# Attention rows of five batches turned into columns through DRAM and DMA transposes in a fused attention and MLP kernel

## The chip, the cores and the metric

The kernel runs on one core of one Trainium2 chip. The metric is the device time of one execution in microseconds (us), as the median of several runs. The core has five engines that run side by side and meet only at semaphores: PE (TensorE, matrix products into eight PSUM banks), ACT (ScalarE), DVE (VectorE), POOL (GpSimd) and SP (SyncE). SP computes nothing here. It issues DMAs, one after the other, and an instruction of SP that waits for a semaphore holds back every DMA behind it. POOL issues DMAs too, on a queue of its own. All DMAs share the core's 16 DMA engines.

## What is computed

Causal attention over 8 batches of 8 heads (576 rows, 64 columns each): the first four heads see the last 32 rows, the other four see every fourth row of the last 128. Its output, 4608 tokens of 512 features, goes through an MLP with 2048 hidden features and a gated activation.

```python
# _attn_ref
scores = scale * np.matmul(q, k.transpose(0, 1, 3, 2))
mask_plain = (rel >= 0) & (rel < window)
mask_dil = (rel >= 0) & (rel < window * dilation) & (rel % dilation == 0)
...
scores = np.where(masks[None, :, :, :], scores, -1000000000.0)
...
attn = attn / (np.sum(attn, axis=-1, keepdims=True) + 1e-09)
return np.matmul(attn, v).astype(np.float32)

# _moe_ref
h = x @ w_in
g = h * (1.0 / (1.0 + np.exp(-beta * h)))
return (g @ w_out).astype(np.float32)
```

## The kernel before

The products run in bf16. The MLP needs the attention output as columns: features on the partitions, tokens along the free axis. That tile is `xT`, 128 partitions by 4 feature blocks `x` (two heads each) by 4608 tokens. Blocks 0 and 1 hold the plain heads, blocks 2 and 3 the dilated ones.

**The MLP** goes over nine token tiles `t` of 512 tokens. For each of 16 blocks of hidden features, `slot_h` makes a slot of four matmuls (L683) from `xT` into a bank, ACT takes its tanh (L690) and DVE multiplies the gate into `g` (L695). `block` then makes the output for 128 tokens in four parts of four matmuls each (L710), ACT or DVE evacuates it to `osb` (L728, L730), and SP stores it (L735). I call a group of four matmuls h*t.n* or o*t.n*: h3.0 is the first slot of tile 3, o2.7 the eighth group of tile 2's output. At most three banks are held by h groups and two by o groups.

**The attention** of a batch makes 14 score groups S (L554, L559, L565), each followed by an exponential on ACT (L592) and, from batch 3 on, by a mask product on POOL or DVE (L604). Then come 12 value groups V (L624), whose rows DVE normalises into a tile `xs` (reciprocal L636, product L637). There are eight `xs` tiles per batch, one for each block `x` and half `j` of the 576 tokens. The function `back` transposes an `xs` tile on PE against the identity (L651, three transposes of 96 rows or four of 72), and `put` copies the bank into `xT` (L205, a helper that serves all copies), on ACT or DVE. The transposes of a batch are named X.

**Loads.** Batches 0 to 2 load q, k and v directly. For batch b from `DIRECT = 3` on, POOL issues two casting DMAs (q and k from float32 to a bf16 DRAM scratch `s`), and SP issues three loads of v (tile `st`, L335) and four DMA transposes from the scratch into `dk`, `dq` and twice `raw` (`crossbar`, L386). POOL and DVE spread these into `qzd`, `kz`, `qd`, `vd` and `vp`. The casts wait for a gate of tile b-2 and for the transposes of batch b-1.

**The order of the work** on every engine is written out in advance by `Plan.run`. Each step has dependencies, estimated costs on the engines that could run it, and a due time `vt` in units of token tiles. The planner keeps a clock for each engine, one for the DMA system and one for each bank, and of the steps that can start within some tens of nanoseconds of the first it takes the one with the earliest due time. A DMA step is counted as landed 1100 ns after its turn in the DMA system. On the chip the planner's times play no part, only the order it chose: every engine runs its list strictly in sequence. Batch b's attention is due during tile b-1, and tile b's h groups need columns of batch b and some of batch b-1. A tile 3 group reads all of batch 3's columns; from tile 4 on, tile t needs only the first half (j = 0) of batch t, beside columns of batch t-1.

Of the kernel before, what the change touches and what calls it, by code (L numbers as in the profile page):

```python
# [9 lines left out]
BF16 = mybir.dt.bfloat16  # L10
# [144 lines left out]
def kernel(  # L155
# [10 lines left out]
    nc = tc.nc  # L166
    P = 128
    B, H, S, D = q.shape
# [6 lines left out]
    C = 4  # L175
# [4 lines left out]
    QT = 96  # L180
# [6 lines left out]
    DIRECT = 3  # L187
# [4 lines left out]
    dram_pool = ctx.enter_context(tc.tile_pool(name="dram", bufs=1, space=bass.MemoryType.DRAM))  # L192
# [4 lines left out]
    plan = Plan(range(8))  # L197
# [6 lines left out]
    def copy(e, out, in_):  # L204
# [15 lines left out]
    xT = const([P, NKT, B * S], BF16, "xT")  # L220
# [6 lines left out]
    xs = {(x, j): const([QT if x < 2 else HT, 3 if x < 2 else C, 2, D], BF16, f"xs{x}{j}")  # L227
          for x in range(4) for j in range(2)}
# [172 lines left out]
    def used(key, o):  # L401
        last.setdefault(key, []).append(o)

    def wrote(*keys):
        for key in keys:
            last[key] = []

    xcopy = {}

    def attention(b, ld, names, vts):  # L410

        steps = {}
# [2 lines left out]
        if b < DIRECT:  # L415
            for n in [x for x in names if x[0] in "KQ"]:
                z, kind, i = "KQ".index(n[0]), n[1], int(n[2])
                vt = vt_of[n]
                g = Group("a")
                if kind == "P":  # L420
# [4 lines left out]
                    r = plan.op([("DVE", 480), ("POOL", 1000), act(1024)], relay, deps, vt)  # L425
                    wrote(("rl", z, i))
                    used(("st", z), r)
                    pieces = [rl[:, z, i, T].rearrange("p h d -> p (h d)") for T in range(R)]
                    tdep = [r]
                else:  # L430
                    src = (ks, qs)[z]
                    pieces = [src[:, 4 + h, (4 * c + 2 * i) * D:(4 * c + 2 * i + 2) * D]
                              for h in range(4) for c in range(2)]
# [32 lines left out]
        else:  # L466
            vt = vt_of["zPRE"]
            ready = {"D": [ld["x", 0, 4]]}
            ops = []
            for hf in range(2):  # L470
                def spread(e, hf=hf):
                    rows = slice(64 * hf, 64 * hf + 64)
                    copy(e, qzd[kv][rows, hf], dq[rows])
                o = plan.op([("DVE", 900), ("POOL", 1150)], spread,
                            [ld["x", 1, 4], late_fill, fill4] + war(("qzd", kv, 0), ("qzd", kv, 1)), vt)
# [5 lines left out]
            for e_ in range(2):  # L481
# [4 lines left out]
                o = plan.op([("POOL", 1200), ("DVE", 1400)], spread, [ld["x", 0, 0], late_fill] + war("kz"), vt)  # L486
# [17 lines left out]
        vt = vt_of["zVAL"]  # L504
# [137 lines left out]
        for name in [n for n in names if n[0] == "X"]:  # L642
            x, j = int(name[1]), int(name[2])
            vt = vt_of[name]
            n, m = (QT, 3) if x < 2 else (HT, 4)
            g = Group("a")

            def back(e, x=x, j=j, g=g, n=n, m=m):
                xp = bank(g, BF16)
                for a in range(m):  # L650
                    nc.tensor.transpose(  # L651
                        xp[:, a * n:(a + 1) * n], xs[x, j][:, a].rearrange("p h d -> p (h d)"),
                        ident_b[0:n, 0:n])
            need = [vdone[x, j]] if x < 2 else [vdone[x, 2 * j], vdone[x, 2 * j + 1]]
            xop = plan.op([("PE", m * mm(n))], back, need, vt, acquire=g)
            wrote(("xs", x, j))
            used(("xs", x, j), xop)

            def put(e, x=x, j=j, g=g):
                xp = bank(g, BF16)[:, 0:S // 2]  # L660
                o = xT[:, x, b * S + j * S // 2:b * S + (j + 1) * S // 2]
                if x >= 2:
                    copy(e, o.rearrange("p (t r) -> p t r", r=C), xp.rearrange("p (r t) -> p t r", r=C))
                elif b < DIRECT:
                    copy(e, o, xp)
                else:
                    copy(e, o.rearrange("p (i m e) -> p i m e", i=3, e=2),
                         xp.rearrange("p (i e m) -> p i m e", i=3, e=2))
            xcopy[b, x, j] = plan.op([act(S // 2), dve(S // 2)], put, [xop], vt - .002, group=g)
# [181 lines left out]
```

## Time and profile before

| | |
|---|---|
| runs | 328.39, 328.99, 329.13 us; median 328.99 us |
| profiled execution | 328.01 us, of which the span of recorded instructions is 326.3 us |
| granted TensorE clock | 1.0 |
| PE | 311.8 us busy, 96% of the span |
| DVE, ACT, POOL | 218.4, 190.2, 107.0 us busy |
| DMA moved | 40.03 MB |

The profile comes from one execution. A page gives busy times by engine, the chain of work that ended last (followed back from the last instruction to whatever released each step), the costliest groups of instructions, and the DMA issues with their time to landing. PE's busy time counts pipelined matmuls, so the chain is the safer reading of what PE takes. "SPq" rows are DMA instructions on SP's queue: their duration is how long SP was held by the instruction, not how long the data took.

### The profile page before, as it was taken

The page shows a single profiled execution, that of the slowest core. Times are in us where ns is not written, and L with a number is a line of the kernel's source. Part 1 is how long each engine was busy: PE and PEld are TensorE (multiplying, and loading weights), DVE is VectorE, ACT ScalarE, POOL GpSimd, SP SyncE. Part 2 cuts the span into 40 slices and gives each one's busy share as a digit, 9 for nine tenths or more (in the row PEclk, how much of TensorE's full clock was granted, in tenths as well). Part 3 has the DMA queues.
Part 4 walks back from the last instruction along what each step waited for, and adds up shares of the span by engine and source line. Part 5 has one row for each costly group of instructions (what it writes and reads, how often), then busy time and mean ns, then how long its engine had stood idle before and what let it go on. Part 6 is the DMA issues. An engine that isn't in the chain of part 4 may idle for free.

```text
span 326.3 us, 6475 instructions
## 1 busy us (share of the span) xinstructions
PE 311.8 (96%) x2445; PEld 176.7 (54%) x2485; DVE 218.4 (67%) x500; ACT 190.2 (58%) x365; POOL 107.0 (33%) x135
## 2 busy tenths in 40 slices
PE   6888999999999998999999999999999999999994
PEld 4766777566555544555555455545554444444441
DVE  5577678778787868887789768876885344344300
ACT  3677778587666656464746574657464544445411
POOL 7999352603542539045405520551000000000000
PEclk9999999999999999999999999999999999999999
DMA  6999999979606892899489457950000010000111
GB/s 85 180 208 208 203 156 176 148 164 228 99 33 140 213 182 87 183 242 167 104 210 188 121 104 176 220 125 32 34 32 34 32 64 35 32 32 34 57 72 64
DMA packets 69614, 40.03 MB, mean 123 GB/s; under 512 B 50816, under 2 KB 64272, under 8 KB 69264
## 3 DMA queue, kind: packets, MB, share of 16 engines
q0 software_dynamic: 20784, 16.09, 35.0%
q1 hardware_dynamic: 48800, 23.54, 32.2%
q8 instruction: 19, 0.31, 0.4%
q14 instruction: 11, 0.09, 0.1%
HBM read 40.37 MB, written 15.34 MB: 171 GB/s over the span
## 4 chain that ended last, share of the span: by engine, by line
PE 85%; DVE 4%; ACT 3%; DMA 3%; issue 2%; POOL 1%; SPq 1%; POOLq 0%; ACTq 0%; DVEq 0%
PE bank L710 36%; PE bank L683 34%; PE bank L624 4%; PE bank L651 3%; PE bank L554 2%; PE bank L394 2%; PE bank L548 2%; PE bank L565 2%; DMA st<-in_k_dram 2%; DMA raw<-s 1%; ACT tnh L690 1%; DVE xs L637 1%; DVE g L695 1%; SPq L386 1%; POOL qd L205 1%
## 5 line engine op out<-in xcount | busy, mean ns | idle before, releaser
L690 ACT ACTIVATE tnh<-bank,beta_half 128x512 bf16<-128x512 f32 (+2 forms) x160 | 102.6, 644 | 90.2 <-PE bank L683 81.8
L683 PE MATMUL bank<-xT,w_in_bf 128*128 128x512 bf16 (+2 forms) x621 | 144.2, 357 | 1.9 <-ACT xT L205 0.3
L710 PE MATMUL bank<-w_out_bf,g 128*128 128x512 bf16 x555 | 141.6, 379 | 1.1
L695 DVE SCALAR_TENSOR_TENSOR g<-tnh,bank 128x512 bf16<-128x512 bf16 (+2 forms) x160 | 100.6, 632 | 60.9 <-ACT tnh L690 59.0
L683 PEld LDWEIGHTS <-w_in_bf 128*128 128x128 bf16 x640 | 58.3, 97 | 49.3 <-issue 2.5
L710 PEld LDWEIGHTS <-g 128*128 128x128 bf16 x576 | 52.2, 98 | 50.3
L592 ACT ACTIVATE pt<-bank 128x288 bf16<-128x288 f32 (+1 forms) x112 | 44.9, 446 | 5.4 <-PE bank L554 2.1
L637 DVE TENSOR_TENSOR xs<-bank,rcp 72x256 bf16<-72x256 f32 (+1 forms) x96 | 44.6, 465 | 3.3
L604 POOL TENSOR_TENSOR pt<-pt,mask_d 128x288 bf16<-128x288 bf16 x15 | 12.0, 808 | 66.9 <-ACT pt L592 66.8
L728 ACT ACTIVATE osb<-bank 128x512 f32<-128x512 f32 (+1 forms) x35 | 20.7, 591 | 17.5 <-PE bank L710 16.6
L624 PEld LDWEIGHTS <-pt 128*128 128x128 bf16 x448 | 22.6, 97 | 12.1 <-issue 0.7
L651 PEld LDWEIGHTS <-xs 72*128 72x128 bf16 (+1 forms) x224 | 15.3, 97 | 13.0 <-DVE xs L637 1.4
L651 PE MATMUL bank<-ident_b,xs 72*128 72x72 bf16 (+1 forms) x224 | 18.8, 200 | 1.2 <-DVE xs L637 0.8
L636 DVE RECIPROCAL rcp<-bank 72x4 f32<-72x4 f32 (+1 forms) x96 | 16.8, 175 | 4.0 <-PE bank L624 2.6
L205 DVE COPY xT<-bank 128x288 bf16<-128x288 bf16 x31 | 13.5, 437 | 7.4 <-PE bank L651 7.3
L205 ACT COPY xT<-bank 128x288 bf16<-128x288 bf16 x33 | 13.1, 397 | 8.4 <-PE bank L651 8.3
L554 PE MATMUL bank<-qzd,dk 128*128 128x144 bf16 x128 | 17.7, 232 | 0.0
L624 PE MATMUL bank<-vd,pt 128*128 128x65 bf16 x256 | 16.2, 193 | 0.3
L205 POOL CAST vd<-st 80x1024 bf16<-80x1024 f32 (+1 forms) x10 | 10.5, 1052 | 15.6 <-DMA st<-in_v_dram 15.2
L554 PEld LDWEIGHTS <-dk 128*128 128x128 bf16 x128 | 11.6, 101 | 5.3 <-issue 0.6
L205 POOL COPY qd<-raw 64x1152 bf16<-64x1152 bf16 x10 | 12.3, 1231 | 1.8 <-PE bank L651 1.6
L604 DVE TENSOR_TENSOR pt<-pt,mask_d 128x288 bf16<-128x288 bf16 x25 | 10.7, 450 | 1.1 <-ACT pt L592 1.1
(96 smaller groups left out, 227.0 us busy)
## 6 DMA issues: line engine op xcount, KB each, us to landing
out_dram<-osb SPq DMA_DIRECT2D x35, 256.0 KB, 2.2
st<-in_v_dram SPq DMA_DIRECT2D x5, 768.0 KB, 8.5
s<-in_k_dram POOLq DMA_DIRECT2D x5, 576.0 KB, 5.6
s<-in_q_dram POOLq DMA_DIRECT2D x5, 576.0 KB, 8.3
st<-in_v_dram SPq DMA_DIRECT2D x5, 512.0 KB, 6.0
w_out_bf<-in_moe_w_out_dram POOLq DMA_DIRECT2D x2, 1024.0 KB, 21.7
st<-in_k_dram POOLq DMA_DIRECT2D x6, 288.0 KB, 9.1
st<-in_q_dram POOLq DMA_DIRECT2D x6, 288.0 KB, 10.6
```

The lines of the kernel that those rows point to most:

```text
L205: (nc.scalar.copy if e == "ACT" else E[e].tensor_copy)(out=out, in_=in_)
L554: nc.tensor.matmul(sc[:, a, 0:2 * n], lhsT=dk[kv][:, rp, h4, hf * (CT - P):hf * (CT - P) + P], rhs=qzd[kv][:, :, rp, h4, hf * HT:(hf + 1) ...
L592: nc.scalar.activation(out=pt_of(x, j, n).rearrange("p (a b) n -> p a b n", a=2), in_=sc[:, :, 0:2 * n].rearrange("p a (b n) -> p a b n", ...
L604: E[e].tensor_tensor(out=w, in0=w, in1=m, op=ALU.mult)
L624: nc.tensor.matmul(pv[:, a, h2, :], lhsT=pt[x][:, c], rhs=rhs, start=True, stop=True)
L637: nc.vector.tensor_tensor(out=xs[x, jx][:, a0:a0 + m], in0=pv[0:n, :, :, 0:D], in1=rc[0:n, 0:m].unsqueeze(3).to_broadcast([n, m, 2, D]), o ...
L651: nc.tensor.transpose(xp[:, a * n:(a + 1) * n], xs[x, j][:, a].rearrange("p h d -> p (h d)"), ident_b[0:n, 0:n])
L683: nc.tensor.matmul(bank(g)[:, 0:n], lhsT=w_in_bf[:, kt, fb * P:(fb + 1) * P], rhs=xT[:, kt, xo:xo + n], start=(kt == 0), stop=(kt == NKT - 1))
L690: nc.scalar.activation(out=th[:, 0:n], in_=bank(g)[:, 0:n], func=ACT.Tanh, scale=beta_half[:, fb:fb + 1])
L695: nc.vector.scalar_tensor_tensor(out=g_t[t % 2][:, fb, c0:c0 + n], in0=th[:, 0:n], scalar=1.0, in1=bank(g)[:, 0:n], op0=ALU.add, op1=ALU.mult)
L710: nc.tensor.matmul(bank(g), lhsT=g_t[t % 2][:, fb, tb * P:(tb + 1) * P], rhs=w_out_bf[:, fb, :], start=(fb == 0), stop=(fb == NFB - 1))
L728: nc.scalar.mul(out=ob[:, cols], in_=bank(g)[:, cols], mul=0.5)
```

## The change

For batches 3 to 7, `back_dma` takes the place of `back` and `put`. An `xs` tile is stored to a DRAM scratch of 288 rows of 128 bf16 (73.7 KB): one store for blocks 2 and 3, two stores for blocks 0 and 1, where even and odd rows lie in different halves of the partitions. Then a DMA transpose brings the scratch into `xT`, after both stores have landed. Both kinds are issued by SP. Batches 0 to 2 keep PE's way. Per batch that is 12 stores and 8 DMA transposes more on SP, 28 PE transposes (8 X groups) and 8 copies fewer; over five batches 60 stores, 40 DMA transposes, 140 PE transposes and 40 copies.

```diff
+    def back_dma(b, x, j, vt, vdone):
+
+        rows = dram_pool.tile([S // 2, P], BF16, name=f"x{b}_{x}{j}")
+        if x < 2:
+            to = rows[:].rearrange("(i m e) c -> e m i c", e=2, m=QT // 2)
+            pieces = [(xs[x, j][e * QT // 2:(e + 1) * QT // 2].rearrange("p a h d -> p a (h d)"), to[e])
+                      for e in range(2)]
+            need = [vdone[x, j]]
+        else:
+            pieces = [(xs[x, j][:].rearrange("p r h d -> p (r h d)"),
+                       rows[:].rearrange("(t r) c -> t (r c)", r=C))]
+            need = [vdone[x, 2 * j], vdone[x, 2 * j + 1]]
+        wrote(("xs", x, j))
+        out = []
+        for src, dst in pieces:
+            o = plan.op([("SP", 450)], lambda e, s=src, d=dst: nc.sync.dma_start(out=d, in_=s), need, vt,
+                        dma=74 * 1000 / len(pieces) / 200)
+            used(("xs", x, j), o)
+            out.append(o)
+        cols = xT[:, x, b * S + j * S // 2:b * S + (j + 1) * S // 2]
+        xcopy[b, x, j] = plan.op(
+            [("SP", 600)], lambda e: nc.sync.dma_start_transpose(out=cols.unsqueeze(1), in_=rows[:]), out,
+            vt, dma=74 * 1000 / 200)
 
     def attention(b, ld, names, vts):
...
         for name in [n for n in names if n[0] == "X"]:
             x, j = int(name[1]), int(name[2])
             vt = vt_of[name]
+            if b >= DIRECT:
+                back_dma(b, x, j, vt, vdone)
+                continue
             n, m = (QT, 3) if x < 2 else (HT, 4)
```

Since the planner runs again, the order moves too, from batch 3 on. In the changed kernel the lines after L409 lie further down: tanh is L717, the evacuation L755, the exponential L616, the store of the output L762, the new store L425 and the new DMA transpose L431.

ACT's list shows where tile 3 begins. Each tanh row is one h group, each `pt` row one S group, each `osb` row four o groups. Before, from the evacuation of o1.11 on (the ninth row is the tanh of h3.0):

```order
L728 ACTIVATE osb_98<-bank_66 128x512
L690 ACTIVATE tnh_92<-bank_70,beta_half 128x512
L205 COPY xT<-bank_67 128x288
L690 ACTIVATE tnh_93<-bank_66,beta_half 128x512
L205 COPY xT<-bank_69 128x288
L690 ACTIVATE tnh_94<-bank_67,beta_half 128x512
L690 ACTIVATE tnh_95<-bank_66,beta_half 128x512
L728 ACTIVATE osb_99<-bank_68 128x512
L690 ACTIVATE tnh_92<-bank_67,beta_half 128x512
L592 ACTIVATE pt_110<-bank_66 128x4x72
L690 ACTIVATE tnh_93<-bank_69,beta_half 128x512
L592 ACTIVATE pt_111<-bank_66 128x4x72
```

The same place now:

```order
L755 ACTIVATE osb_98<-bank_65 128x512
L717 ACTIVATE tnh_92<-bank_68,beta_half 128x512
L717 ACTIVATE tnh_93<-bank_70,beta_half 128x512
L717 ACTIVATE tnh_94<-bank_68,beta_half 128x512
L717 ACTIVATE tnh_95<-bank_70,beta_half 128x512
L755 ACTIVATE osb_99<-bank_71 128x512
L616 ACTIVATE pt_110<-bank_70 128x4x72
L616 ACTIVATE pt_111<-bank_65 128x4x72
L616 ACTIVATE pt_110<-bank_66 128x4x72
L616 ACTIVATE pt_111<-bank_67 128x4x72
L755 ACTIVATE osb_96<-bank_68 128x512
L616 ACTIVATE pt_110<-bank_65 128x4x72
```

The copies into `xT` are gone, and the tanh of h3.0 has moved behind 17 further rows: batch 4's 14 exponentials and three evacuations (o2.3, o2.7, o2.11). After it 13 tanh rows of tile 3 follow one another. The beginnings of tiles 5 and 6 have moved back in the same way, by a few groups of the tile before and some of the next batch's scores. Tiles 7 and 8 alternate h and o as before.

SP's list at the loads of batch 4, before:

```order
L735 DMA out_dram<-osb_96 128x512
L735 DMA out_dram<-osb_97 128x512
L335 DMA st_120<-in_v_dram 80x4x256
L335 DMA st_120<-in_v_dram 128x4x256
L335 DMA st_121<-in_v_dram 128x24x64
L386 DMA_TRANSPOSE dk_129<-s_0_138 128x2x576
L386 DMA_TRANSPOSE dq<-s_1_139 128x2x576
L386 DMA_TRANSPOSE raw<-s_0_138 128x1x1152
L386 DMA_TRANSPOSE raw<-s_1_139 128x1x1152
```

And now (x_20 is the scratch of block 2, half 0):

```order
L762 DMA out_dram<-osb_96 128x512
L425 DMA x_20_138<-xs_116 72x512
L425 DMA x_30_139<-xs_118 72x512
L335 DMA st_120<-in_v_dram 80x4x256
L335 DMA st_120<-in_v_dram 128x4x256
L335 DMA st_121<-in_v_dram 128x24x64
L431 DMA_TRANSPOSE xT<-x_20_138 128x1x288
L386 DMA_TRANSPOSE dk_129<-s_0_146 128x2x576
L386 DMA_TRANSPOSE dq<-s_1_147 128x2x576
L386 DMA_TRANSPOSE raw<-s_0_146 128x1x1152
L386 DMA_TRANSPOSE raw<-s_1_147 128x1x1152
L431 DMA_TRANSPOSE xT<-x_30_139 128x1x288
```

Two new stores stand ahead of batch 4's loads and one new DMA transpose ahead of its crossbar transposes; the store of `osb_97` has moved behind them. The other columns of batch 3 follow after that: 14 more of the new DMAs and three stores of the output, and then, last:

```order
L762 DMA out_dram<-osb_96 128x512
L425 DMA x_20_148<-xs_116 72x512
L762 DMA out_dram<-osb_97 128x512
L431 DMA_TRANSPOSE xT<-x_01_144 128x1x288
L431 DMA_TRANSPOSE xT<-x_11_145 128x1x288
```

Here batch 3's last two DMA transposes, which h3.0 waits for, stand behind a store of batch 4's rows (x_20_148) and behind the store of the output groups o2.4 to o2.7 (`osb_97`). Before, nothing of the kind stood on SP there: from `raw` to batch 5's loads its list had three stores of the output.

## The prediction

> **What bounds the kernel now.** I read the page's busy times first, then its chain that ended last.
>
> ```profile
> PE 311.8 (96%) x2445; PEld 176.7 (54%) x2485; DVE 218.4 (67%) x500; ACT 190.2 (58%) x365; POOL 107.0 (33%) x135
> PE 85%; DVE 4%; ACT 3%; DMA 3%; issue 2%; POOL 1%; SPq 1%; POOLq 0%; ACTq 0%; DVEq 0%
> ```
>
> PE holds 85% of the chain, so a group of matmuls taken off PE is worth its full time unless something else is late. Whether something is late differs by stage, so next I asked for busy times in stretches of 15 us (columns: PE, PEld, DVE, ACT, POOL, clock, DMA share, GB/s).
>
> ```profile
> 120.00:135.00 15.00, 13.99 (x100) 7.28 (x100) 12.51 (x24) 9.27 (x18) 9.53 (x10) 1.00 0.65 132
> 165.00:180.00 15.00, 14.84 (x131) 8.29 (x133) 13.73 (x34) 8.60 (x17) 4.60 (x5) 1.00 1.03 203
> 180.00:195.00 15.00, 14.89 (x101) 7.76 (x102) 10.85 (x23) 9.12 (x18) 6.48 (x7) 1.00 0.45 109
> 255.00:270.00 15.00, 14.89 (x69) 6.80 (x70) 5.71 (x10) 7.38 (x11) 0.00 (x0) 1.00 0.09 35
> ```
>
> In the stages that the change touches PE is busy 14.84 to 14.89 us of 15, as it is in the stage without attention (255 to 270), with one exception: about 0.9 us are lost between 120 and 135. DVE and ACT are never full. So PE binds, and every reduction of its work counts.
>
> **What the change takes off PE.** The chain in order of time has the X groups one by one (start, us, what).
>
> ```profile
> 160.30 0.17 PE bank L565 x4
> ...
> 173.10 0.12 PE bank L554 x2
> ...
> 175.29 0.12 PE bank L624 x4
> ...
> 180.41 0.13 PE bank L651 x4
> 180.55 0.86 PE bank L683 x4
> 181.41 0.13 PE bank L651 x3
> 181.54 0.19 PE bank L624 x6
> ```
>
> An X group takes 0.13 us between its neighbours, whether of four 72-row or three 96-row transposes, and an h group 0.86 (S groups take 0.12 or 0.17, V groups 0.12 or 0.19; I use these below). Eight X groups in each of five batches are 40 x 0.13 = 5.2 us. All lie on the bounding engine: I take -5.2.
>
> **The copies.** The 40 copies into `xT` cost some 0.4 us each, 17 us in all:
>
> ```profile
> L205 DVE COPY xT<-bank 128x288 bf16<-128x288 bf16 x31 | 13.5, 437 | 7.4 <-PE bank L651 7.3
> L205 ACT COPY xT<-bank 128x288 bf16<-128x288 bf16 x33 | 13.1, 397 | 8.4 <-PE bank L651 8.3
> ```
>
> ACT and DVE have that time free beside PE, so I count 0. What hides it is PE's work; should another engine set the pace, the copies' absence helps by at most that one's share.
>
> **What it adds: SP.** SP gets 60 stores and 40 DMA transposes. The stores' nearest row is the store of the output, which holds SP 332 ns and lands in 2.0 us; for the new DMA transposes it is `raw`, four times their size.
>
> ```profile
> L735 SPq DMA_DIRECT2D out_dram<-osb x37: 332/332/537, 58.4 to 322.7; - x37
> L386 SPq DMA_TRANSPOSE raw<-s x10: 1194/1530/3010, 81.0 to 211.4; - x10
> L386 SPq DMA_TRANSPOSE dk<-s x5: 5582/5694/9456, 73.8 to 201.9; - x5
> L386 SPq DMA_TRANSPOSE dq<-s x5: 1247/1304/2507, 79.5 to 208.4; - x5
> DMA to landing us min/median/max: 1.7/2.0/8.1
> raw<-s SPq DMA_TRANSPOSE x10, 4.1
> ```
>
> (The three figures are minimum, median and maximum in ns; the last two rows give us to landing, of the output's stores and of `raw`.) A store I take at 0.35 us of SP and 2 us to landing. A DMA transpose of 74 KB lies between a quarter of `raw` (0.3 to 0.4 us) and all of it (1.5 us). I take 0.4, because SP's time on `raw` goes with the data: 295 KB in 1.3 us is 227 GB/s, about the rate at which the DMA engines run at that time. Landing I take at 2.5 us, between the quickest store, 1.7, and `raw`, 4.1, which are the ends, and nearer the former by its size.
>
> The row that worries me is `dk`: the same size as `dq`, yet SP is held 5.7 us instead of 1.3. It is always the first DMA transpose after v's loads. In SP's timeline (start, us):
>
> ```profile
> 105.71 4.66 SPq L335 DMA_DIRECT2D st<-in_v_dram  x3
> 110.47 5.58 SPq L386 DMA_TRANSPOSE dk<-s  x1
> 116.22 2.51 SPq L386 DMA_TRANSPOSE dq<-s  x1
> 118.83 3.05 SPq L386 DMA_TRANSPOSE raw<-s  x2
> 121.97 1.05 SPq L735 DMA_DIRECT2D out_dram<-osb  x2
> ```
>
> Either SP waits there until v's 1.6 MB have drained, or the change from copies to transposes costs 4.4 us by itself. In 110.47 to 116.05 the DMA engines are busy without a break:
>
> ```profile
> 110.50:116.00 5.50, 5.45 (x51) 2.95 (x50) 4.93 (x13) 2.58 (x5) 3.10 (x4) 1.00 1.19 268
> st<-in_v_dram SPq DMA_DIRECT2D x5, 768.0 KB, 8.5
> ```
>
> 268 GB/s for 5.5 us is 1.47 MB, nine tenths of v's three loads (768 KB in the row, with 320 and 512). So I take the first reading, and 0 for the change of kind; 4.4 us is the other end, and the slower rival below.
>
> **The waits that it makes.** New orders put SP's DMAs ahead of PE's work at two kinds of place. The first is h3.0. The chain around it before:
>
> ```profile
> 115.52 0.20 PE bank L624 x6
> 118.83 4.04 DMA raw<-s
> 126.40 1.29 POOL qd L205
> 127.73 0.33 PE bank L565 x4
> ```
>
> V3.11 (the last values of batch 3) is the first row, and S4.4 (batch 4's first plain scores) the last, which waited 0.9 us for POOL's `qd`, that for `raw`. In the new order PE reaches V3.11 about 0.8 us earlier (six X groups less). From there stand o1.12 to o2.2 with three h groups (ten groups, 8.6 us), S4.0 to S4.3 (0.5), o2.3 to o2.6 with three V groups (3.9), S4.4 to S4.7 (0.7) and o2.7 (0.9): it ends at 114.9 + 14.6 = 129.5. ACT then evacuates it (0.6 us, behind two exponentials: done by 130.5), SP stores it (0.35), issues batch 3's last two DMA transposes (0.8), and they land by 134. PE meanwhile has five o groups, six S and eight V groups, 4.3 + 0.8 + 1.1 = 6.2 us, and wants h3.0 at 135.7. That leaves 1.7 us, if SP is free at 130.5. It should be: after the loads (122) come 10 stores, 5 DMA transposes and three output stores, about 6.5 us, ending near 128.5 with no wait on a landing longer than 2 us. With 1.5 us per DMA transpose it ends at 134, and h3.0 is 2 to 3 us late.
>
> S4.4 is the second kind: the loads. Its wait of 0.9 us stays, since one DMA transpose now stands before `dk` on SP, for which X groups no longer run. I count 0 there. Batch 5's casts wait for the gate of h3.4, now ten groups later; from h3.4 to S5.0 PE has 27 h and o groups, 23 us. v's loads wait for the gate of h3.6. From their first issue to the end of the spreads the trace of before has, in its slowest and its quickest batch:
>
> ```profile
> 132.24 1.79 SPq L335 DMA_DIRECT2D st<-in_v_dram  x3
> ...
> 151.36 1.15 POOL L205 COPY qzd<-dq 64x1152 bf16<-64x1152 bf16 x1 [3.58 <-DMA dq<-s]
> ...
> 154.10 2.82 POOL L205 COPY qd<-raw 64x1152 bf16<-64x1152 bf16 x2
> ...
> 197.07 4.71 SPq L335 DMA_DIRECT2D st<-in_v_dram  x3
> ...
> 212.56 1.15 POOL L205 COPY qzd<-dq 64x1152 bf16<-64x1152 bf16 x1 [1.70 <-DMA dq<-s]
> ...
> 215.50 1.14 POOL L205 COPY qd<-raw 64x1152 bf16<-64x1152 bf16 x1
> ```
>
> That is 17 to 20 us to `qzd`, which S5.0 needs, and 20 to 25 to `qd`, which S5.4 needs. The gate of h3.6 comes 3 us after that of h3.4, so S5.0 has a margin of 1 to 4 us and S5.4, 2 us later in PE's list, 0 to 3. Batches 6 and 7, counted in the same way, have 3 to 6. What shortens these margins is DMA traffic: 74 KB go out and come back 40 times, 5.9 MB on top of 40.03, mostly between the bursts of the loads, where the share is 0.45. During casts it is worse: the output's slowest store, 8.1 us to landing where 2.0 is the median, was issued at 131.8, two us after a pair of casts. For all of these I allow +1.2 us: the places with a margin of 0 to 2 us are two (h3.0, S5.4), their ends are 0 and 3 us each, and my times lie nearer the lower. Below nothing is possible too: without the wait at S4.4 (-0.9).
>
> Last, 13 h groups now follow one another in tile 3, three banks at a time. A bank's round is 0.86 on PE, then tanh and gate:
>
> ```profile
> L690 ACT ACTIVATE tnh<-bank,beta_half 128x512 bf16<-128x512 f32 x128 | 88.0, 687 | 85.8 <-PE bank L683 77.6 <-remote 3.9 <-DVE rcp L636 1.4
> L695 DVE SCALAR_TENSOR_TENSOR g<-tnh,bank 128x512 bf16<-128x512 bf16 x128 | 87.6, 685 | 56.7 <-ACT tnh L690 55.3
> ```
>
> 0.86 + 0.69 + 0.69 and some 0.1 of hand-overs is 2.34 us, under three slots of PE (2.58). It holds while DVE and ACT do little else, and there they do: 0, at most 0.2 x 13 / 3 = 0.9.
>
> **The sum.** -5.2 + 1.2 + 0 = -4.0 us. The profiled execution took 328.01 us (span 326.3), so it would be 324.0. The median of the runs lies 1.0 above it, at 328.99: 325.0.
>
> **A rule against the change.** The Trainium skill, VectorE: DVE Perf Modes, section The three transpose paths, gives 390 ns for a 128 x 128 bf16 transpose on TensorE and 1309 ns on the DMA crossbar, and its rules for authors prefer TensorE where PSUM will do. This trace has both sides differently: 0.13 us for three or four on PE, and `raw`, nine such blocks, in 1.53 us of SP and 4.1 to landing, where the page would give 11.8. By the page's figure each new DMA transpose would be an estimated 2.9 us, and the sum an estimated 45 us of loss, as worked out from a row in the third rival below.
>
> **The rivals.**
> 1. *The waits eat the gain.* X stores fall into the casts and take 8 us instead of 2, so that h3.0, h5.0 or h6.0, or the scores of batch 5, wait for xT or the loads. One place costs 6 us less its margin of 2 to 3: 3 to 4. One or two places bring the sum to between -2 and +2, and the time to 327 to 331, say 328.5. For it: DMA shares of 1.03 in the bursts. Against: SP issues in sequence, so most of the new DMAs fall between the bursts.
> 2. *SP becomes the bound: slower.* If a DMA transpose after a copy holds SP 4.4 us longer, as `dk`'s row can be read, three such changes (after the loads: to x_00, to x_21, to x_01) add 13 us ahead of h3.0 and it waits 11. Tiles 5 and 6 begin behind as many. 325 + 2 x 11 = 347, with all three 358. It decides from 0.6 us a change upwards (3 x 0.6 exceeds the 1.7 of margin), and turns the sum positive from about 2. For it: 5.58 to 5.69 three times of five looks like a constant. Against: the DMA engines full at that moment.
> 3. *DMA transposes are slow in themselves: slower.* At the longest `raw` row, 3.0 us of SP each, eight make 24 us a batch; with 16 us for the loads (105.71 to 121.97) and 12 stores of 0.35, SP needs 44 us for a tile in which PE needs 32 groups of 0.86 and 4 us of attention, 32. That is 12 us in each of tiles 3 to 6, 48 in all: 373 us. Against: `raw`'s median is half of that for four times the data.
> 4. *Nothing waits at all,* S4.4 included: -5.2 - 0.9, 322.9 us. For it: tile 7 reads columns whose values stand some 20 groups ahead of it; against: the margins above.
>
> **Chances.** The forecast, 0.54, and rival 4, 0.08, between them 322.3 to 326.8. Rival 1, 326.8 to 331: 0.22. Over 331, rival 2: 0.13, rival 3: 0.03. The range from 322.3 to 331 leaves out these two and the tails, 2 in 10. A measurement of this kernel can tell about 0.2% (0.66 us) from no change; rival 1 crosses that band, and I split it 0.08, 0.07, 0.07. Faster: 0.70; the same: 0.07; slower: 0.16 + 0.07 = 0.23.
>
> **What would show it.** Right: no L651 rows after 100 us; the store holds SP about 0.35 us and the DMA transpose about 0.4, landing in 2 to 3; PE busy at 14.8 of 15 us from 130 on; the chain still PE from 130 to the end. Wrong: a DMA transpose of 1.3 us or more on SP; PE idle before h3.0, h5.0 or h6.0, released by a DMA into `xT`; PE idle before S5.4 or S6.0, released by POOL's `qd` or `kz`.

## The result and the profile after

The changed kernel takes 340.36 us in the median of four runs (338.80 to 341.75), the kernel before 329.06 (328.39 to 329.17): a ratio of 1.0346, 95% interval 1.0299 to 1.0394. It is slower by 11.3 us where 325.0 was forecast and 331 was the upper end. The profiled execution, the slowest of the four, took 341.75 us with a span of 340.1, so the difference to explain in the traces is 340.1 - 326.3 = 13.8 us. Executions in the chip's slower state are left out of the times below (two of `casts_held`, one each of `stores_on_act` and `casts_rows_4096`).

The page after: busy times, the chain that ended last, and the row of the h groups (busy us and mean ns, then idle time ahead and what ended it).

```profile
PE 311.4 (92%) x2308; PEld 171.8 (51%) x2345; DVE 208.0 (61%) x462; ACT 183.0 (54%) x347; POOL 119.4 (35%) x151
PE 77%; DMA 7%; DVE 4%; ACT 4%; SPq 3%; issue 3%; POOL 1%; ACTq 0%; POOLq 0%
L710 PE MATMUL bank<-xT,w_in_bf 128*128 128x512 bf16 (+2 forms) x623 | 146.3, 365 | 14.9 <-DMA xT<-x 12.7
```

PE's share of the chain fell from 85% to 77%, and the h groups stood idle for 12.7 us behind DMAs into `xT`. That is the sign that the prediction had named for "wrong". In stretches of time (columns as before), first one of the kernel before, then the changed kernel:

```profile
135.00:150.00 15.00, 14.84 (x132) 8.30 (x133) 12.56 (x33) 9.22 (x18) 4.41 (x4) 1.00 1.20 205
```

```profile
120.00:135.00 15.00, 14.89 (x140) 8.54 (x140) 12.40 (x31) 7.34 (x18) 11.77 (x13) 1.00 0.49 120
135.00:150.00 15.00, 4.52 (x21) 1.66 (x18) 2.13 (x6) 1.28 (x2) 0.01 (x1) 0.61 0.80 169
146.60:156.00 9.40, 9.35 (x31) 3.71 (x33) 4.08 (x6) 4.62 (x7) 0.00 (x0) 0.71 0.39 102
225.00:240.00 15.00, 13.70 (x95) 7.11 (x96) 10.61 (x17) 6.56 (x14) 9.08 (x7) 1.00 0.87 162
240.00:255.00 15.00, 12.68 (x74) 6.13 (x74) 8.65 (x20) 7.96 (x15) 2.30 (x3) 0.89 0.42 115
```

Nearly all of it is lost in one place, and behind it the granted clock is 0.71 for 9.4 us. The loss: 10.5 us of PE idle ahead of h3.0, 9.4 x 0.29 = 2.7 us of clock behind it, 0.6 us at 180 to 184, 3.5 us of waits at 236 to 243 (2.3 of them for columns of tile 6) and 15 x 0.11 = 1.7 us of clock behind those: 19.0. The X groups that are gone give 5.2 back, the wait of 0.9 us at S4.4 is gone too, and 12.9 of the 13.8 us are found.

The place itself, in the chain, in SP's list and in POOL's list (start, us, what):

```profile
136.18 0.60 ACT osb L755
...
136.98 9.46 DMA xT<-x
```

```profile
129.29 2.39 SPq L431 DMA_TRANSPOSE xT<-x  x2
131.72 3.06 SPq L425 DMA_DIRECT2D x<-xs  x3
134.88 0.86 SPq L762 DMA_DIRECT2D out_dram<-osb  x2
135.83 0.57 SPq L425 DMA_DIRECT2D x<-xs  x1
136.53 0.34 SPq L762 DMA_DIRECT2D out_dram<-osb  x1
136.98 8.44 SPq L431 DMA_TRANSPOSE xT<-x  x2
```

```profile
131.32 2.69 POOL L628 TENSOR_TENSOR pt<-pt,mask_d 128x288 bf16<-128x288 bf16 x3
133.96 0.55 POOL L335 DMA_DIRECT2D s<-in_k_dram  x1
134.50 0.50 POOL L335 DMA_DIRECT2D s<-in_q_dram  x1
```

The chain puts the evacuation of o2.11 (136.18) ahead of SP here, but SP's store at 136.53 is that of `osb_97`, which was evacuated by 130.86, and it took its usual 0.34 us: SP was late by its own list. SP has hardly a pause and reaches batch 3's last two DMA transposes at 137.0, where the prediction had 130.9. By then POOL has issued batch 5's casts, at once behind its last masks of batch 4. The second transpose has to wait until its own stores have landed and is issued at 144.3, and PE starts h3.0 at 146.57. Both queues between 136 and 141 us (packets, MB, share of 16 engines):

```profile
q0 software_dynamic: 63, 0.87, 105.3%
q1 hardware_dynamic: 75, 0.02, 2.3%
```

The software queue (the casts) has the DMA engines to itself; SP's queue moves 0.02 MB in 5 us. The new instructions (minimum, median, maximum of SP's time in ns), and in the list of DMAs the transposes' median landing in us:

```profile
L425 SPq DMA_DIRECT2D x<-xs x60: 312/434/3335, 102.7 to 266.2; - x60
L431 SPq DMA_TRANSPOSE xT<-x x40: 1105/1152/4972, 109.2 to 268.1; - x40
```

```profile
xT<-x SPq DMA_TRANSPOSE x40, 2.4
```

### The profile page after: what moved, and what is told of

Read it like the earlier page. It is cut to its first block, busy times and chain, and to the rows that moved or that the text cites. A ratio compares the mean times of both kernels' runs of the same rounds, so it can differ in the third digit from the quotient of the medians.

```text
span 340.1 us, 6311 instructions
## 1 busy us (share of the span) xinstructions
PE 311.4 (92%) x2308; PEld 171.8 (51%) x2345; DVE 208.0 (61%) x462; ACT 183.0 (54%) x347; POOL 119.4 (35%) x151
## 3 DMA queue, kind: packets, MB, share of 16 engines
q0 software_dynamic: 20784, 16.09, 33.5%
## 4 chain that ended last, share of the span: by engine, by line
PE 77%; DMA 7%; DVE 4%; ACT 4%; SPq 3%; issue 3%; POOL 1%; ACTq 0%; POOLq 0%
PE bank L710 35%; PE bank L737 32%; DMA xT<-x 4%; PE bank L648 3%; DMA st<-in_q_dram 3%; PE bank L578 2%; SPq L386 2%; PE bank L572 1%; DVE xs L661 1%; PE bank L394 1%; ACT pt L616 1%; ACT tnh L717 1%; PE bank L589 1%; DVE g L722 1%; SPq L425 1%
## 5 line engine op out<-in xcount | busy, mean ns | idle before, releaser
L710 PE MATMUL bank<-xT,w_in_bf 128*128 128x512 bf16 (+2 forms) x623 | 146.3, 365 | 14.9 <-DMA xT<-x 12.7
L717 ACT ACTIVATE tnh<-bank,beta_half 128x512 bf16<-128x512 f32 (+2 forms) x160 | 102.6, 644 | 102.1 <-PE bank L710 95.7
L737 PE MATMUL bank<-w_out_bf,g 128*128 128x512 bf16 x556 | 139.6, 379 | 1.0
L710 PEld LDWEIGHTS <-w_in_bf 128*128 128x128 bf16 x640 | 61.0, 99 | 73.2 <-issue 18.5
L616 ACT ACTIVATE pt<-bank 128x288 bf16<-128x288 f32 (+1 forms) x112 | 43.1, 449 | 12.7 <-PE bank L578 9.0
L628 POOL TENSOR_TENSOR pt<-pt,mask_d 128x288 bf16<-128x288 bf16 x26 | 20.1, 786 | 37.9 <-ACT pt L616 31.7
L755 ACT ACTIVATE osb<-bank 128x512 f32<-128x512 f32 (+1 forms) x34 | 20.1, 592 | 24.0 <-PE bank L737 19.7
L648 PEld LDWEIGHTS <-pt 128*128 128x128 bf16 x448 | 22.8, 98 | 13.9 <-issue 1.7
L205 POOL CAST vp<-st 128x1536 bf16<-128x1536 f32 x5 | 7.3, 1466 | 11.2 <-DMA st<-in_v_dram 9.2
L648 PE MATMUL bank<-vp,pt 128*128 128x65 bf16 x192 | 10.8, 197 | 0.2
L757 DVE TENSOR_SCALAR osb<-bank 128x512 f32<-128x512 f32 (+1 forms) x3 | 1.8, 600 | 13.8 <-ACT osb L755 13.7
L205 POOL COPY kz<-raw 64x1152 bf16<-64x1152 bf16 x5 | 8.1, 1614 | 3.8 <-DMA raw<-s 3.6
L572 PEld LDWEIGHTS <-ident_b 128*128 128x128 bf16 x84 | 8.5, 101 | 0.8
## 6 DMA issues: line engine op xcount, KB each, us to landing
st<-in_q_dram POOLq DMA_DIRECT2D x6, 288.0 KB, 10.5
```

Of the source, the lines that this page charges most:

```text
L205: (nc.scalar.copy if e == "ACT" else E[e].tensor_copy)(out=out, in_=in_)
L616: nc.scalar.activation(out=pt_of(x, j, n).rearrange("p (a b) n -> p a b n", a=2), in_=sc[:, :, 0:2 * n].rearrange("p a (b n) -> p a b n", ...
L628: E[e].tensor_tensor(out=w, in0=w, in1=m, op=ALU.mult)
L648: nc.tensor.matmul(pv[:, a, h2, :], lhsT=pt[x][:, c], rhs=rhs, start=True, stop=True)
L710: nc.tensor.matmul(bank(g)[:, 0:n], lhsT=w_in_bf[:, kt, fb * P:(fb + 1) * P], rhs=xT[:, kt, xo:xo + n], start=(kt == 0), stop=(kt == NKT - 1))
L717: nc.scalar.activation(out=th[:, 0:n], in_=bank(g)[:, 0:n], func=ACT.Tanh, scale=beta_half[:, fb:fb + 1])
```

## The experiments

Two theories stood against each other at first: PE loses what it waits for columns, or the new order of the work costs by itself. For late columns there were two candidates, SP's time per transpose and the casts.

**columns_free** takes the DMAs away and keeps the order.

```diff
-    ... lambda e, s=src, d=dst: nc.sync.dma_start(out=d, in_=s), need, vt,
+    ... lambda e: None, need, vt,
-    ... lambda e: nc.sync.dma_start_transpose(out=cols.unsqueeze(1), in_=rows[:]), out,
+    ... lambda e: nc.gpsimd.memset(cols, .01), out,
```

> The changed kernel's order on every engine, but the 60 stores and 40 DMA transposes of batches 3 to 7 are left out, and POOL fills those columns of xT with a constant where the transposes stood (so the attention of batches 3 to 7 does not reach the output). Nothing waits for columns or for SP's extra DMAs. Theory W (the order is innocent, the time goes into waits for columns that arrive late): PE keeps its 5.2 us of gain and the kernel takes 323 to 326 us. Rival O (the new order itself, with attention bunched up and 13 h groups in a row, costs the time): 333 to 341 us, with PE idle again ahead of h3.0, or ACT and DVE ahead of PE.

323.74 us, 0.9836 of before (0.9804 to 0.9869): 5.4 us faster. The order is innocent, and the prediction's term of -5.2 for 40 X groups was right.

**copy_not_transpose** keeps stores, waits and bytes, and only replaces the transpose by a plain copy.

```diff
-    ... lambda e: nc.sync.dma_start_transpose(out=cols.unsqueeze(1), in_=rows[:]), out,
+    ... lambda e: nc.sync.dma_start(out=cols, in_=rows[:].rearrange("a c -> (a c)").rearrange("(p n) -> p n", p=P)), out,
```

> The changed kernel with each of the 40 new DMA transposes replaced by a plain DMA of the same scratch into the same columns of xT (rows and columns are not exchanged). Order, waits and bytes stay. Theory S (SP is late at h3.0's last two transposes because each transpose holds it 1.15 us, so that these fall behind batch 5's casts): a plain DMA holds SP 0.35 to 0.4 us, six of them ahead of h3.0 free it about 4.5 us earlier, the last columns leave ahead of the casts or with them, PE's wait at h3.0 falls from 10.5 to under 4 us, and the kernel takes 328 to 333. Rival C (the casts alone decide: whatever is in flight or issued from 134 us on lands 8 us late): the wait stays 8 to 10 us and the kernel at 337 to 341.

323.71 us, 0.9832 (0.9801 to 0.9863), as if there were no DMAs at all, and better than theory S expected. SP's time per copy, and the last two copies ahead of h3.0:

```profile
L431 SPq DMA_DIRECT2D xT<-x x40: 326/384/4387, 110.0 to 247.8; - x40
```

```profile
131.92 1.22 SPq L431 DMA_DIRECT2D xT<-x  x2
```

A copy holds SP 0.38 us, 0.77 less than the transpose, and SP comes to the last pair at 131.9, five us sooner and ahead of the casts (here at 134.6). The copy lands in 2.2 us, the transpose in 2.4 (medians), so landing in quiet is not the difference. SP's list behind v's loads for batch 4, where a plain copy now stands ahead of `dk`:

```profile
109.98 3.78 SPq L431 DMA_DIRECT2D xT<-x  x1
113.86 1.42 SPq L386 DMA_TRANSPOSE dk<-s  x1
```

**copy_and_two_small** gives SP its time back without any transpose: behind each copy two DMAs of 256 bytes.

```diff
+    ...
+        for i in range(2):
+            nc.sync.dma_start(out=small[n[0]:n[0] + 1], in_=rows[0:1])
+            n[0] += 1
```

> The columns come back by plain copies, as in copy_not_transpose (323.7 us), but two DMAs of 256 bytes from DRAM to DRAM follow each, so that SP is held about as long for a set of columns as the DMA transpose holds it (0.33 + 2 x 0.38 = 1.1 us against 1.11). As there, the columns of batches 3 to 7 are wrong in content. Theory S (what costs is SP's time, 1.1 us forty times, which brings SP to the last two sets ahead of h3.0 at 137 instead of 132, into batch 5's casts): the wait of h3.0 is back, 8 to 11 us of PE idle at 136 to 147, and the time is 335 to 342. Rival D (what costs is the transpose's own way through the DMA engines, its landing or its read of DRAM, and not SP's time): no wait at h3.0, 324 to 327.

355.39 us, 1.0802 (1.0766 to 1.0838): the loss is back, and larger than expected. SP's times, and the chain ahead of h3.0:

```profile
L415 SPq DMA_DIRECT2D small<-x x80: 467/578/1452, 114.1 to 292.2; - x80
L413 SPq DMA_DIRECT2D xT<-x x40: 326/434/5669, 109.5 to 291.1; - x40
```

```profile
133.39 10.92 DMA xT<-x
...
144.32 0.02 SPq L433
...
146.81 3.46 DMA xT<-x
```

A set, here one copy with its two small DMAs, holds SP 0.43 + 2 x 0.58 = 1.6 us instead of 1.15. SP is late again, and a plain copy that goes out beside the casts takes 10.9 us. Then SP stands from 139.9 to 144.3, until that copy has landed, and the last copy ahead of h3.0 leaves only at 146.8. This adds to the overshoot, so the run is not a test of SP's time alone. What it shows is that the loss needs no transposing: plain copies meet the casts as well when SP comes late. Together with `copy_not_transpose` it makes the time on SP, not the transposing, what the DMA transpose brings the loss by.

**casts_held** makes POOL wait for the first gate of tile b-2 before it issues batch b's casts: for batch 5 that of h3.0. (The prediction believed that these casts waited for the gate of h3.4.)

```diff
+        ...
+            if z == 0 and b > DIRECT:
+                nc.gpsimd.tensor_copy(out=hold[:], in_=g_t[(b - 2) % 2][:, 0, 0:1])
```

> The changed kernel with one 128x1 copy on POOL ahead of each pair of casts of batches 4 to 7, reading the first gate of tile b-2, so that batch 5's casts really wait for h3.0's gate, as the planner meant them to. Theory C (the casts hold the stores and transposes back): the last two transposes before h3.0 land in 2.4 us instead of 7.8, PE's wait there falls from 10.5 to 4 to 5 us (SP still reaches them at 137, and needs 1.15 us for each), the clock drops less, and the kernel takes 330 to 335, if batch 5's loads, now some 10 us later, do not take the gain back ahead of S5.0. Rival S (SP's own time decides, casts are harmless): the wait stays at 9 to 10.5 and the kernel at 339 to 344.

337.79 us, 1.0259 (1.0187 to 1.0330), so theory C missed the total. The wait for h3.0 falls from 10.5 to 3.5 us, but the later casts make the loads late, and PE loses 1.8 to 2.9 us in each of three later stretches of 15 us. **casts_5_out** leaves that price out, with batch 5's casts.

```diff
+        if b == 5:
+            scratch[b, z] = scratch[b - 1, z]
+            return plan.op([("POOL", 750)], lambda e: None, deps, vt, dma=1152 * 1024 / .38 / 1000)
```

> The changed kernel without the two casts of batch 5 (2.36 MB that POOL's queue brings through the DMA engines); batch 5 reads the scratch of batch 4, so that its attention is that of batch 4's q and k with its own v. The order is the same. Theory K (two parts: SP comes late to the last columns, which alone costs h3.0 3 to 4 us, and the casts, which hold these columns back until they are done at 144, cost the other 6 to 7 and the slower clock behind them): the wait ahead of h3.0 is 3 to 4 us, the time 340.4 less 6.6 and 1 to 3 of clock, 330 to 333. Rival (SP's lateness alone makes the whole wait, the casts only lie beside it): 10 us stay, and the time is 338 to 341.

335.06 us, 1.0189 (1.0151 to 1.0227): the wait as expected, the total 2 us above the expected span, because tiles 5 and 6 still wait for their columns. The chain and PE ahead of h3.0 (in brackets the idle time and what ended it):

```profile
137.74 2.36 DMA xT<-x
```

```profile
138.96 0.38 PE L713 MATMUL bank<-xT,w_in_bf 128*128 128x512 bf16 x1 [2.63 <-DMA xT<-x]
140.15 12.17 PE L713 MATMUL bank<-xT,w_in_bf 128*128 128x512 bf16 x47 [0.81 <-DMA xT<-x]
```

So h3.0's 10.5 us are two parts: 3.4 by SP's late arrival alone, 7.1 by the casts. The second needs the first: in `copy_not_transpose`, with the casts in place and SP early, h3.0 waits for nothing.

**Three ways to relieve SP.** `stores_on_act` issues the 60 stores from ACT's queue (`nc.scalar.dma_start`), `merged` brings back two blocks with one transpose of 148 KB, `priced` tells the planner the measured time.

```diff
 # stores_on_act
-    ... lambda e, s=src, d=dst: nc.sync.dma_start(out=d, in_=s), need, vt,
+    ... lambda e, s=src, d=dst: nc.scalar.dma_start(out=d, in_=s), need, vt,
 # merged
-    rows = dram_pool.tile([S // 2, P], BF16, ...)
+    rows = dram_pool.tile([S // 2, 2, P], BF16, ...)     # for a pair of blocks
+    [("SP", 1200)], lambda e: nc.sync.dma_start_transpose(out=cols, in_=rows[:].rearrange("a x c -> a (x c)")), stores,
 # priced
-    [("SP", 600)], lambda e: nc.sync.dma_start_transpose(...
+    [("SP", 1150)], lambda e: nc.sync.dma_start_transpose(...
```

> The 60 stores into the scratch are issued by ACT's queue instead of SP's, in the same places of the planner's order; the DMA transposes stay on SP. Theory S: ten stores of 0.43 us ahead of h3.0 leave SP, so that it comes to the last two transposes about 4 us sooner, at 132 to 133, ahead of the casts or with them: PE's wait for h3.0 falls from 10.5 to between 0 and 4 us, and the time to 326 to 334 (ACT has 0.3 us per store to spare in most stages). Rival D (the landing of stores and transposes beside the casts, whoever issues them): the wait stays at 8 us or more, 337 to 342. Rival A (ACT stands behind a store that waits, and PE's banks with it): PE waits for ACT's tanh or evacuations, over 340.

> Two blocks share one scratch of 288 x 2 x 128 values, and one DMA transpose brings back both: 20 transposes of 148 KB instead of 40 of 74 KB; 60 stores as before; the planner prices them at 1200 ns, so that rows may move. Theory S with a fixed time per transpose (1.1 us for 74 KB, 1.2 to 1.5 for raw's 295 KB): each holds SP 1.1 to 1.25 us, four transposes less stand ahead of h3.0 and SP comes there 4 us sooner; the wait falls to 0 to 4 us and the time to 325 to 331. If SP's time goes with the data instead (2.2 us each), nothing is won: 337 to 342.

> The planner is told 1150 ns of SP for a DMA transpose, as measured, instead of 600, and orders the program anew (rows move from the end of batch 3's attention on: the last values come ahead of some o and h groups). If the loss is a wrong price that the planner could have planned around: h3.0 comes later in PE's list, with o groups ahead of it, and the time is 326 to 332. If the order cannot hide forty transposes on one queue beside the casts, which the planner does not see: 334 to 342.

339.70 us, 1.0329 (1.0301 to 1.0357); 337.65, 1.0273 (1.0237 to 1.0309); 340.49, 1.0334 (1.0289 to 1.0379). The first two miss what theory S expected of them. From the chain of `stores_on_act`, the chain of `merged`, and SP's time in `merged`:

```profile
134.62 9.45 DMA xT<-x
```

```profile
135.24 9.43 DMA xT<-x
```

```profile
L436 SPq DMA_TRANSPOSE xT<-x x20: 1192/1228/2289, 120.5 to 261.5; - x20
```

The part of the theory on time holds: twice the data holds SP 1.23 us instead of 1.15, so the time is nearly fixed per instruction. What it left out is that coming a few us sooner brings little here. All three still come to the last columns within 2.5 us of the casts, and these land with the casts' end, so that h3.0 starts at 144.1, 144.8 and 146.1 instead of 146.6. It waits 5.6, 7.5 and 6.6 us; that is less than 10.5 mostly because PE itself comes there later (138.5, 137.3 and 139.5 instead of 136.1). On ACT the stores also stand behind the exponentials, and a store that waits holds back ACT: it computes nothing from 134.7 to 144.6. In three other places PE waits for evacuations on ACT, 4.3 us in all, which it does nowhere in the changed kernel; so rival A of the expectation holds in part. Only `copy_not_transpose`, with its last two copies at 131.9 and 132.8 and the casts at 134.6, is clear. The price is a step, not a slope.

**Fewer sets.** A set is the columns of one `xs` tile. `late_halves` sends 20 of the 40 sets through DRAM: the second halves of batches 4 to 6 and all of batch 7. `late_merged` is the same with merged pairs. `late_24` adds the first half of batch 4 only; `from_batch_4` takes all of batches 4 to 7.

```diff
-            if b >= DIRECT:
+            if b > DIRECT and (j == 1 or b == B - 1):              # late_halves
+            if b > DIRECT and (b < 5 or j == 1 or b == B - 1):     # late_24
+            if b > DIRECT:                                         # from_batch_4
```

> The new path only where the columns are wanted a tile later: the second halves (j = 1) of batches 4 to 6, and all of batch 7; batch 3 and the first halves of 4 to 6 keep PE's transposes. 20 of 40 X groups are off PE, worth 2.6 us at 0.13 each. Theory W: no group waits for a column, the order stays that of before (h and o alternate from tile 3 on), and the kernel takes 326 to 328 us, 1 to 3 less than before. Rival L (stores held back by casts keep SP from the next batch's loads of v, and the scores come late): 329 to 334, with PE idle ahead of a batch's first scores.

> merged and late_halves together: 10 transposes of 148 KB for the second halves of batches 4 to 6 and both halves of batch 7, TensorE for the others. Theory S: late_halves (325.5 us) had no long wait left, so ten transposes less on SP win little, 324.5 to 326; if a pair's transpose, which waits for the later of its two blocks, makes PE wait in places, 326 to 329.

> late_halves with the first half of batch 4 as well: 24 sets by the scratch. late_halves left PE idle for 0.2 us or less in each stretch of 15 from 135 on, so four X groups less are worth 0.5 us: 325.0 (324.5 to 325.4). If the four additional sets make h4.0 wait: over 326.

> Batch 3's columns go by TensorE again, those of batches 4 to 7 by the scratch (32 of 40 sets). If each place stands by itself: the wait at h3.0 and the clock behind it go (-13.2), 8 X groups come back (+1.0), the 5.8 us lost at 180 to 184 and 236 to 250 stay: 340.4 - 13.2 + 1.0 = 328, 327 to 330. If the later waits came only of the first: 329 - 32 x 0.13 = 324.8, 324.5 to 326.

`late_halves`: 325.50 us, 0.9880 (0.9842 to 0.9917), 1.2% faster than the kernel before and 0.5 us better than the range expected. `late_merged`: 326.01, 0.9904 (0.9884 to 0.9923), no better. `late_24`: 342.98, 1.0413 (1.0383 to 1.0442), 17 us slower than `late_halves` for four sets more. `from_batch_4`: 343.66, 1.0421 (1.0385 to 1.0458). Both of the last miss by far, on the other side: without batch 3 the loss did not go, it moved. SP's list in `late_24`, one of SP's waits (us in total, times, longest), and PE ahead of the next tile's h groups:

```profile
134.06 2.24 SPq L425 DMA_DIRECT2D x<-xs  x2
141.68 1.11 SPq L431 DMA_TRANSPOSE xT<-x  x1
142.88 1.01 SPq L425 DMA_DIRECT2D x<-xs  x2
143.98 1.59 SPq L335 DMA_DIRECT2D st<-in_v_dram  x3
```

```profile
SPq L431 <- DMA x<-xs: 5.3, 1, 5.3
```

```profile
172.92 5.70 PE L710 MATMUL bank<-xT,w_in_bf 128*128 128x512 bf16 x15 [7.67 <-DMA xT<-x]
```

Batch 4's stores fall into the casts of batch 5 (here at 131.0) and land late; the transpose behind them waits 5.3 us on SP, and v's loads for batch 5 stand behind it. In `late_halves` they stand ahead of every new DMA (SP's list, then PE in stretches):

```profile
133.09 1.75 SPq L335 DMA_DIRECT2D st<-in_v_dram  x3
```

```profile
150.00:165.00 15.00, 14.89 (x94) 7.58 (x95) 10.36 (x22) 9.34 (x18) 7.64 (x8) 1.00 0.73 149
165.00:180.00 15.00, 14.84 (x127) 8.22 (x129) 13.25 (x34) 8.26 (x16) 4.31 (x5) 1.00 1.06 226
```

Eleven us of delay to v's loads delay batch 5's scores, with them its columns, and these meet batch 6's casts at 163.8. PE in `late_halves` is full in every stretch from 135 on.

**Why the casts hold back SP's queue.** Between 136 and 141 us the two queues' packets were about one to one by number, 13.8 KB each against 0.3. Three kernels change only how the casts walk over their data: rows of 128, rows of 4096, and 96 x 12 rows of 256 values that lie apart.

```diff
-    dst[:].rearrange("x (a e) -> (x a) e", e=1024)       # and src alike
+    dst[:].rearrange("x (a e) -> (x a) e", e=128)        # casts_rows_128; casts_rows_4096 with e=4096
+    dst[:].rearrange("x n -> (x n)").rearrange("(b a e) -> a b e", b=12, e=256)   # casts_scattered
```

> The casts move the same 2.36 MB in rows of 128 values instead of 1024; nothing else changes. From 136 to 141 us the changed kernel's software queue brought 63 packets of 13.8 KB on average, and the hardware queue 75 of 0.3 KB: about one to one by number. Theory P (the DMA engines take turns by packet, so that a packet of the casts costs each small packet of SP's queue its length): if the casts' packets become shorter, the columns' DMAs get through the casts, the landing of the last transposes falls from 9.5 to 3 to 6 us and PE's wait for h3.0 from 10.5 to 3.5 to 7 us, 328 to 336, unless the casts themselves take much longer. Rival B (it is the bytes, or the casts' hold on DRAM, not the packets): the wait stays at 9 us or more, 338 to 345.

> The casts in rows of 4096 values instead of 1024. Theory P: packets of the same size or longer, and the wait for h3.0 the same or longer, 10 to 13 us, 339 to 346. Rival B: no difference from the changed kernel, 338 to 342.

> The casts go over the same values in another order, 96 times 12 rows of 256 values that lie apart, so that the rows cannot be joined; the rows' length alone changed nothing in casts_rows_128 and casts_rows_4096 (20784 packets of the software queue in both, as in the changed kernel). Theory P (the DMA engines take turns by packet): more and shorter packets of the casts, the last transposes land sooner than 9.5 us after their issue, and PE waits 3.5 to 7 us for h3.0, if the casts do not take over twice their 9.4 us. Rival B (bytes): the columns land with the end of the casts, whenever that is, and PE waits 10 us or more; with longer casts the time is 340 to 370.

341.58 us, 1.0357 (1.0287 to 1.0427), and 340.95, 1.0312 (1.0210 to 1.0414). The packets were the same 20784 in both, so these say nothing on packets; they are two further runs of the changed kernel in effect. `casts_scattered`: 338.59, 1.0297 (1.0264 to 1.0329), with 31984 packets. Its queues between 136 and 141 us:

```profile
q0 software_dynamic: 1069, 0.54, 90.4%
q1 hardware_dynamic: 229, 0.44, 25.9%
```

Packets of 0.5 KB instead of 13.8 let 0.44 MB of SP's queue through in the same 5 us, instead of 0.02. That agrees with a rule of the Trainium skill, DMA: Bandwidth & Descriptors, section Queues, rings and completion order: each DMA engine takes turns between its queues packet by packet. But PE's wait stayed at 10.9 us. The stores landed sooner (the last transpose went out at 139.1 instead of 144.3), and then that transpose landed 8.1 us later instead of 2.3, as the casts now lasted 13.9 us instead of 9.4. So theory P fits the runs on who gets the engines, and was wrong that this would save the wait; that the bytes in the way are the same would explain it, but is not shown apart. (The last store of these columns also left SP 0.4 us sooner than in the changed kernel, so the packets are not the only difference.)

## Why the prediction was wrong

- **What bounds the kernel, and the gain.** Right. -5.2 us was forecast for the X groups, and with columns that cost nothing 5.4 are measured. The copies' absence gave nothing beyond that, as said.
- **SP's time for a DMA transpose: the step that failed first.** 0.4 us was taken "because SP's time on `raw` goes with the data". It is 1.15 us for 74 KB, 1.23 for 148, and 1.2 to 1.5 for `raw`'s 295. The bounds, a quarter of `raw` and all of it, held; the value was taken at the wrong end. (The 1.3 us in its rate of 227 GB/s is `dq`'s time; `raw`'s own median is 1.53.) All DMA transposes of the profile before had one size, 295 KB, so its rows could not tell a fixed time from one in proportion, and between ends so far apart the choice decided. By the Trainium skill's figure, which the prediction names as a rule against the change (VectorE: DVE Perf Modes, section The three transpose paths), a new DMA transpose would be an estimated 2.9 us. This trace has 1.15 us on SP and 2.4 us to landing.
- **h3.0.** o2.7 ended at 129.51, as forecast, and its evacuation at 130.86. SP should have reached the store at 130.5, "with 1.5 us per DMA transpose" at 134 and h3.0 2 to 3 us late. Without the casts it came there at 135.65 and h3.0 was 3.4 us late. That these two agree is in part luck. With the measured 1.15 us the prediction's count (10 stores, 5 DMA transposes, 3 output stores) ends at 132.3. It left out two stores that stand there in SP's list (`osb_96` and x_20), a store took 0.43 us and not 0.35, some 0.05 us lie between two DMAs, and one store of the output held SP 1.14 us.
- **"Batch 5's casts wait for the gate of h3.4": the step that failed worst.** The casts wait for that gate in the planner's dependencies and order only. On POOL nothing holds them but their place in its list, behind the last masks of batch 4, which this order puts ahead of h3.0. So they fell at 134.0 on top of the last columns, and not 10 us behind them. That is 7.1 of the 10.5 us, and the clock behind a longer idle time.
- **Rival 1, "the waits eat the gain",** had the mechanism, x stores in the casts with 8 us to landing. Its price of 3 to 4 us a place was too low by a factor of three, since it set against it a margin that SP had already used up, and left the clock out.
- **Rival 2** read `dk`'s 5.7 us as the price of a transpose after a copy. In the profile after, `dk` holds SP 1.32 us where a new transpose stands between it and v's loads, and that one takes 4.91: the time belongs to the first DMA behind the loads, whichever it is. In `copy_not_transpose` a plain copy stands there, and `dk` behind it, now the change from copies to transposes, is held no longer (3.78 and 1.42 us). The prediction was right to count 0 for the change of kind, and rival 2 gave a time of its size for another reason.
- **S4.4, S5.0, S5.4.** S4.4's wait of 0.9 us, which was to stay, is gone (PE is busy 14.89 us of 15 between 120 and 135). The loads' margins in the changed kernel held for S5.0 and S5.4, which wait for nothing; batch 7's scores wait 0.6 us for `qd` at 237, where a margin of 3 to 6 us had been counted. In the two kernels where a transpose stands ahead of v's loads (`late_24`, `from_batch_4`) they did not hold.
- **The banks in a row of 13 h groups** cost nothing that shows.

## What to carry to other kernels

A DMA transpose cost its issuing queue 1.15 us for 74 KB and 1.23 for 148: count instructions, not bytes. Merging pairs took 2.7 us off the changed kernel, and nothing off `late_halves`. A store, its landing and a second DMA on a queue that also issues loads make each wait a wait of the loads; put such round trips behind the loads in the list, and use them only for columns that are needed a tile later (20 of 40 sets brought 1.2%, four more sets, with columns needed in the very next tile, cost 5%). And a dependency of a planner holds nothing back on the chip: look up which semaphore or which instruction ahead in its list holds a large transfer, and where it falls when the rest moves.

## What the runs showed of the hardware that was not expected

- A burst of casting DMAs (two of them, 2.36 MB read; 9.4 us from the second one's issue to its landing) all but stops SP's queue: 0.02 MB in 5 us. Transfers of up to 74 KB that went out within 3 us behind its issue, and some that went out 1 us ahead of it, were in place only 7 to 11 us later, copies as well as transposes; the medians over the kernel are 2.2 us for a copy and 2.4 for a transpose. With shorter packets of the casts SP's queue moved 22 times as much in that time.
- An idle time of 10.5 us cost 2.7 us more afterwards: the granted clock was 0.61 in it and 0.71 in the 9.4 us behind it. With 3.4 us of idle time (`casts_5_out`) the stretch of 15 us around it has 0.89.
- Rows that lie one behind the other make the same packets whatever length of row the kernel writes down: 20784 with rows of 128, 1024 and 4096 values.
